# Attention and a maxout feed-forward on one core: the order in which the weights are prepared, and the engine that scales p in the first two batches

## The chip, the cores and the metric

The kernel runs on one core of one Trainium2 chip. The metric is the device time of one execution in microseconds (us); lower is better. The time before is the median of three runs, 803.49 us (803.19 to 803.58).

## The reference

Eight batches of eight-head attention over 576 positions, with a window of 128 keys and a linear bias by distance, and then a feed-forward layer on all 4608 tokens, whose hidden value is the largest of three products. Cut to what matters:

```python
scores = scale * np.matmul(q, k.transpose(0, 1, 3, 2))         # q, k, v: (8, 8, 576, 64)
bias = slopes[:, None, None] * (-np.abs(rel).astype(np.float32))[None, :, :]
scores = np.where((rel >= 0) & (rel < 128), scores + bias[None], -1000000000.0)
attn = np.exp(scores - np.max(scores, axis=-1, keepdims=True))
attn = attn / (np.sum(attn, axis=-1, keepdims=True) + 1e-09)
x = np.matmul(attn, v) -> (4608, 512)
h = np.maximum(np.maximum(x @ w1, x @ w2), x @ w3)              # w1, w2, w3: (512, 768)
return h @ w_out                                                # w_out: (768, 512)
```

## The kernel before

**Attention.** The work is cut into tasks (a batch and a pair of heads, `t` = 0 to 31, four to a batch) and steps (128 queries of a task, `s` = 0 to 159, five to a task, the fifth with 64 queries). For a pair of steps `products` (L314) makes the scores on the tensor engine (PE). For each step `score` masks them on the vector engine (DVE, L329 or L332), adds the bias and finds the row minimum of the negated scores (DVE, L344), and takes exp on the scalar engine (ACT, L348), which leaves p and its row sums. `sums_of` turns the sums into reciprocals on DVE (L357, L360), into the tile `st`. `normalise` multiplies p by them: before the change on ACT, one instruction for each head of a step (L367). `turn` transposes p on PE (L376), copies it out of PSUM on ACT (L380, L386, L389), and GpSimd (POOL) cuts the two triangles out of it (L390, L394). `mix` multiplies with v on PE (L416), and after a task's last step ACT copies the result into `xk` (L425).

**Feed-forward.** It runs one batch behind attention. Batch 0 is multiplied plainly, in 88 units (`plain_unit`, L585): 8 for each of 12 groups of weights. Groups 0 to 8 are the thirds of w1, w2, w3 for one part p of the hidden rows; groups 9 to 11 are w_out. Its operand `xs` is cut from `xk` (ACT L442, DVE L443) when all of batch 0's attention is done. The outputs of groups 0 to 8 are merged by `put`: the first third of a part is copied by ACT (L546), the others are max-ed by DVE (L544). Batches 1 to 7 run a scheme with seven products in place of eight (`unit`, L623); it needs sums and differences of the weights, which `add` and `add_part` make on DVE (L195, L153) from a copy of the weights in device memory, `w32`.

**Preparing the weights.** The weights come in as 64-bit values. The generator `preparing` walks over the groups in the order of the table `A_ORDER`, four steps to a group: two of `convert` (ACT L138 and L142, DVE L139, L143 and L148 for each, and a store to `w32`, L149), and two of `part` (a high and a low half by ACT L152 and DVE L153; into the ring `wt` for groups 0 to 8, which the plain units read, and into the constant tiles `ow` for groups 9 to 11). The ring has room for three groups, so the parts of groups 3 to 8 wait until the plain units have used up the group that stands three before. After that come 36 steps of `add` and `add_part` in the order of `B_ORDER`. `weights(n, upto)` takes n steps, and more if fewer than `upto` are done. It is called once at each attention step by the loop at L691 and L692 (s = 1 to 25), and by the units: one step at every second plain unit, and as many as the unit's own group needs (L569).

**What sets the order.** All calls are put into one list of events with a time in steps (L641 to L692) and emitted in that order; the framework's scheduler then moves instructions within each engine, until the `fix` event in batch 2 holds PE's to the written order. Each engine works through its own instructions in order. SP issues the loads and stores.

Of the kernel before, what the change touches and what calls it, by code (L numbers as in the profile page):

```python
# [13 lines left out]
ALU = mybir.AluOpType  # L14
# [15 lines left out]
def attention_maxout_kernel(  # L30
# [11 lines left out]
    nc = tc.nc  # L42
    P = 128
    B, NP, _, _, S = qk.shape
# [41 lines left out]
        out=prev, in_=prev, pattern=[[1, P]], compare_op=ALU.is_gt, fill=0.0,  # L86
# [42 lines left out]
    def fetch(g):  # L129
        for j in range(2):  # L130
            raws[g, j] = hs_p.tile([P, 2 * DM], I32, name="hs2", bufs=4)
            nc.sync.dma_start(raws[g, j], w_all[g, j].bitcast(I32))
# [82 lines left out]

        return (n - RING, 6 if a else 3) in used

    A_ORDER = [0, 1, 2, 9, 10, 11, 3, 4, 5, 6, 7, 8]
    B_ORDER = [0, 1, 2, 9, 10, 11, 3, 4, 5, 6, 7, 8]

    def preparing():
        fetch(A_ORDER[0])
        fetch(A_ORDER[1])
        for n, g in enumerate(A_ORDER):
            for j in range(2):
                convert(g, j)
                yield
            while 3 <= g < 9 and (g - 3, "plain") not in used:
                yield True
            for c in range(2):  # L230
                part(g, c)
                yield
            if n + 2 < NG:
                fetch(A_ORDER[n + 2])
        for g in B_ORDER:
            while g < 2 and (8, "plain") not in used:
                yield True
            while 2 <= g < 9 and not ahead(9 + g, 1):
                yield True
            while g >= 9 and (10, "plain") not in used:  # L240
                yield True
            add(g)
            yield
            for a in range(2):
                add_part(g, a)
                yield
# [5 lines left out]
    def weights(n=0, upto=0):  # L252

        nonlocal prepared
        while n > 0 or prepared < upto:
            stuck = next(steps_of_weights, True)
            if stuck:
                assert prepared >= upto or prepared == STEPS, (prepared, upto)
                return
            prepared += 1  # L260
            n -= 1
# [100 lines left out]
    def normalise(t, i):  # L362
        n = rows[i]
        st, two = stats[t, i // 2]
        for a, p in enumerate(two):
            for j in range(2):
                nc.scalar.activation(p[:n, j], p[:n, j], AF.Copy, scale=st[:n, 2, a, j:j + 1])  # L367

# [192 lines left out]
    def plain_unit(v):  # L561
# [6 lines left out]
        i, j = ij = ((0, 0), (0, 1), (1, 0), (1, 1))[o]  # L568
        weights(r % 2, 4 * (A_ORDER.index(g) + 1) if g < 9 else 48)  # L569
        if g < 9:  # L570
# [70 lines left out]
    def at(when, what, *args):  # L641
        events.append((when, len(events), what, args))
# [3 lines left out]
    for t, (b, hp) in enumerate(tasks):  # L646
        for i in range(NB):
            s = t * NB + i + shift[b]
            if i == LOAD_I and t + 2 < len(tasks):
                at(s - 0.4, load, t + 2)  # L650
            if i == NB - 1 and t + 1 < len(tasks):
                at(s - 0.4, load_v, t + 1)
            if i == 0 and 0 < t < NP:
                at(s - 1, slopes, t)
            c = s - (t * NB + i) % 2

            if s == c:
                at(c + 0.002, products, t * NB + i)
                at(c + LAG_T + 0.003, turn, t * NB + i)
            at(s + 0.04, score, t, i)  # L660
            if i % 2 or i + 1 == NB:
                at(s + 0.9, sums_of, t, i)
                at(s + 1.3, normalise, t, i)
            e = t * NB + next(min(e + 1, NB - 1) for e in GROUPS if e >= i)
            at(e - e % 2 + shift[b] + LAG_X + 0.001, mix, t, i)
# [23 lines left out]
    for u in range(77 * B, 77 * B + 3):  # L689
        at(when, unit, u)  # L690
    for s in range(1, n_steps + LAG_X):  # L691
        at(s + 0.2, weights, 1)  # L692

    def fix():
        nonlocal fixed
# [48 lines left out]
```

## Time and profile before

| | before |
|---|---|
| median of three runs | 803.49 us |
| profiled execution, its own time | 799.82 us |
| its span, from first to last instruction | 797.7 us |
| PE busy | 759.2 us (95%) |
| weight loads of PE busy | 674.2 us (85%) |
| DVE busy | 559.9 us (70%) |
| ACT busy | 531.3 us (67%) |
| POOL busy | 166.8 us (21%) |

The profile shows one execution; its rows name the line of the kernel, the engine, the operation, the tile written and read, and the shapes. Busy time counts the time in which at least one instruction of the engine runs; two neighbours overlap a little, so busy time and count give the duration of one instruction, and the distance from start to start gives what one costs an engine that is never idle. An engine's wait is put down to what released it last. In the strip of 40 slices a digit is a tenth of 20 us. Line numbers are those of the kernel before; below the changed lines those of the kernel after are 5 to 6 higher.

### The profile page before, as it was taken

The page shows a single profiled execution, that of the slowest core. Times are in us where ns is not written, and L with a number is a line of the kernel's source. Part 1 is how long each engine was busy: PE and PEld are TensorE (multiplying, and loading weights), DVE is VectorE, ACT ScalarE, POOL GpSimd, SP SyncE. Part 2 cuts the span into 40 slices and gives each one's busy share as a digit, 9 for nine tenths or more (in the row PEclk, how much of TensorE's full clock was granted, in tenths as well). Part 3 has the DMA queues.
Part 4 walks back from the last instruction along what each step waited for, and adds up shares of the span by engine and source line. Part 5 has one row for each costly group of instructions (what it writes and reads, how often), then busy time and mean ns, then how long its engine had stood idle before and what let it go on. Part 6 is the DMA issues. An engine that isn't in the chain of part 4 may idle for free.

```text
span 797.7 us, 18112 instructions
## 1 busy us (share of the span) xinstructions
PE 759.2 (95%) x6344; PEld 674.2 (85%) x6344; DVE 559.9 (70%) x1897; ACT 531.3 (67%) x1736; POOL 166.8 (21%) x374
## 2 busy tenths in 40 slices
PE   4776998999999999999999999999999999999987
PEld 2434987998888998899989999898988999899987
DVE  5677888488999757793777747793777747673662
ACT  6888888568878656775667657676667667552332
POOL 1221111111214122221223122221222122201100
PEclk7756999999999999999999999999999999999999
DMA  8775785387899459864887459864788458755951
GB/s 282 266 243 171 228 302 208 115 297 231 318 329 314 166 196 320 286 215 138 285 295 252 162 187 323 282 234 136 277 285 257 160 195 288 245 198 195 301 181 60
DMA packets 53771, 187.96 MB, mean 236 GB/s; under 512 B 5936, under 2 KB 14896, under 8 KB 46768
## 3 DMA queue, kind: packets, MB, share of 16 engines
q0 software_dynamic: 15552, 99.10, 37.6%
q1 hardware_dynamic: 37984, 87.64, 32.0%
q8 instruction: 50, 0.82, 0.4%
q14 instruction: 41, 0.34, 0.1%
q10 hardware_dynamic: 144, 0.07, 0.0%
HBM read 154.53 MB, written 32.24 MB: 234 GB/s over the span
## 4 chain that ended last, share of the span: by engine, by line
PE 65%; DVE 12%; issue 9%; ACT 6%; DMA 4%; POOL 2%; SPq 0%; POOLq 0%; ACTq 0%; DVEq 0%
PE ps_m L623 44%; PE ps_x L416 6%; PE ps_m L585 6%; PE ps_s L314 5%; PE pt L376 4%; DMA wt<-keep 2%; ACT p L348 2%; DVE hs L443 2%; DVE xs L443 2%; DMA hs<-in_w_all 1%; DVE t L549 1%; DVE s L344 1%; DVE ps_s L332 1%; DVE hq L550 1%; ACT xs L442 1%
## 5 line engine op out<-in xcount | busy, mean ns | idle before, releaser
L623 PE MATMUL ps_m<-xs,wt 128*128 128x288 f32 x2646 | 370.4, 297 | 4.1 <-DMA wt<-keep 1.7
L623 PEld LDWEIGHTS ps_m<-xs,wt 128*128 128x128 f32 x2646 | 355.4, 188 | 7.9 <-DVE t L549 3.8
L390 POOL TENSOR_SCALAR_AFFINE_SELECT pp<-pr 128x256 f32<-128x256 f32 (+1 forms) x128 | 54.7, 428 | 401.9 <-ACT pr L389 220.2
L348 ACT ACTIVATE p<-s,st 128x128 f32<-128x128 f32 (+1 forms) x320 | 127.0, 399 | 16.0 <-DVE st L344 14.6
L632 ACT COPY t<-ps_m 128x288 f32<-128x288 f32 x231 | 89.7, 394 | 71.2 <-PE ps_m L623 70.8
L623 PE MATMUL ps_m<-hs,ow 128*128 128x288 f32 x882 | 124.0, 297 | 1.6 <-DVE hs L443 0.8
L367 ACT ACTIVATE p<-p,st 128x128 f32<-128x128 f32 (+1 forms) x320 | 110.5, 396 | 19.4 <-DVE st L360 19.4
L623 PEld LDWEIGHTS ps_m<-hs,ow 128*128 128x128 f32 x882 | 118.7, 188 | 3.1 <-ACT t L632 1.2
L270 POOL DMA_DIRECT2D wt<-keep x108 | 58.3, 539 | 194.3 <-PE ps_m L623 187.7
L344 DVE CUSTOM_DVE_ANT_0 s<-ps_s,bias 128x128 f32<-128x128 f32 (+1 forms) x300 | 76.7, 281 | 17.4 <-PE ps_s L314 13.6
L416 PE MATMUL ps_x<-pp,v 128*64 128x256 f32 (+3 forms) x768 | 81.3, 339 | 3.7 <-POOL pp L390 3.6
L332 DVE COPY_PREDICATED ps_s<-prev,ps_s 128x256 f32<-128x256 uint8 x120 | 50.8, 423 | 46.2 <-PE ps_s L314 44.7
L549 DVE TENSOR_TENSOR t<-ps_m,t 128x288 f32<-128x288 f32 x126 | 56.5, 452 | 36.3 <-PE ps_m L623 24.2
L314 PE MATMUL ps_s<-qk 64*64 64x192 f32 (+1 forms) x1080 | 70.2, 336 | 9.2 <-DVE st L344 5.0
L416 PEld LDWEIGHTS ps_x<-pp,v 128*64 128x64 f32 (+1 forms) x768 | 46.1, 142 | 29.9 <-issue 10.6
L442 ACT CAST hs<-hq 128x288 fp32r<-128x288 f32 x117 | 49.0, 430 | 31.9 <-DVE hq L550 16.5
L376 PE MATMUL pt<-ident,p 128*128 128x128 f32 (+1 forms) x320 | 59.2, 296 | 11.2 <-ACT p L367 7.1
L376 PEld LDWEIGHTS pt<-ident,p 128*128 128x128 f32 (+1 forms) x320 | 34.8, 146 | 40.3 <-issue 18.9
L585 PE MATMUL ps_m<-xs,wt 128*128 128x288 f32 x432 | 63.3, 306 | 3.3 <-DVE xs L443 2.6
L585 PEld LDWEIGHTS ps_m<-xs,wt 128*128 128x128 f32 x432 | 60.6, 196 | 4.2 <-DVE xs L443 3.0
L314 PEld LDWEIGHTS ps_s<-qk 64*64 64x64 f32 x1080 | 41.1, 138 | 26.7 <-issue 10.5
L389 ACT COPY pr<-pt 128x256 f32<-128x256 f32 x64 | 18.9, 321 | 66.5 <-PE pt L376 66.5
(58 smaller groups left out, 849.4 us busy)
## 6 DMA issues: line engine op xcount, KB each, us to landing
wt<-keep POOLq DMA_DIRECT2D x54, 1024.0 KB, 7.3
wt<-keep POOLq DMA_DIRECT2D x54, 768.0 KB, 5.5
qk<-in_qk SPq DMA_DIRECT2D x31, 576.0 KB, 5.8
hs<-in_w_all SPq DMA_DIRECT2D x24, 512.0 KB, 5.0
v<-in_v SPq DMA_DIRECT2D x32, 320.0 KB, 4.6
keep<-wt SPq DMA_DIRECT2D x36, 256.0 KB, 3.8
outT<-t SPq DMA_DIRECT2D x64, 144.0 KB, 1.8
wt<-keep SPq DMA_DIRECT2D x27, 256.0 KB, 4.2
```

The lines of the kernel that those rows point to most:

```text
L270: nc.gpsimd.dma_start(wts[n, a], keep[n % 9][a])
L314: pe(nc.tensor.matmul(ps[j][d:d + D, o:o + k1 - k0], lhsT=qkt[t][j * D:(j + 1) * D, 0, q0:q0 + D], rhs=qkt[t][j * D:(j + 1) * D, 1, k0:k1] ...
L332: nc.vector.copy_predicated(both[:, :, P:], mask.unsqueeze(1).broadcast_to([n, 2, P]), both[:, :, :P],)
L344: nc.vector.tensor_tensor_reduce(out=s[:n], in0=ps[j][:n, P:2 * P], in1=(bias if i else bias0)[:n, 2 * hp + j, :], scale=-0.125, scalar=3. ...
L348: nc.scalar.activation(p[:n, j], s[:n], AF.Exp, bias=st[:n, 0, a, j:j + 1], scale=-1.0, accum_out=st[:n, 1, a, j:j + 1])
L367: nc.scalar.activation(p[:n, j], p[:n, j], AF.Copy, scale=st[:n, 2, a, j:j + 1])
L376: pe(nc.tensor.transpose(out=pt[:, a, j, :n], in_=p[:n, j], identity=ident[:n, :n]))
L416: pe(nc.tensor.matmul(x[j * D:(j + 1) * D, c:c + e - a], lhsT=vv[:n, i, j * D:(j + 1) * D], rhs=w[:n, j].rearrange("p a b -> p (a b)")[:, ...
L549: nc.vector.tensor_tensor(out=s, in0=ps, in1=e, op=ALU.add)
L585: pe(nc.tensor.matmul(ps, lhsT=lt, rhs=rt, start=m == 0 and c == 0, stop=m == len(pairs) - 1, skip_group_check=True,))
L623: pe(nc.tensor.matmul(ps, lhsT=lt, rhs=rt, start=i == 0 and k in (0, 1, 4), stop=i == len(pairs) - 1, skip_group_check=True,))
L632: nc.scalar.copy(out=e, in_=ps)
```

## The change

Three edits. (1) `A_ORDER`, the order in which the groups of weights are prepared, becomes 0 to 11; before, groups 9 to 11 stood between 2 and 3. (2) The preparing step at each attention step stops after s = 11; before, it went on to s = 25, so that 25 steps (groups 0, 1, 2, 9, 10, 11 and one step of group 3) were asked for in the first 25 attention steps, and now 11 are (groups 0 and 1 and three of the four steps of group 2). The rest is asked for by the plain units. (3) For the tasks of the first two batches (`t < 2 * NP`) p is scaled on DVE, by one multiplication for both heads of a step, with the reciprocals of `st` broadcast along the row; the other batches keep the two ACT instructions.

```diff
-    A_ORDER = [0, 1, 2, 9, 10, 11, 3, 4, 5, 6, 7, 8]
+    A_ORDER = [0, 1, 2, 3, 4, 5, 6, 7, 8, 9, 10, 11]
...
         for a, p in enumerate(two):
+            if t < 2 * NP:
+                nc.vector.tensor_tensor(
+                    out=p[:n], in0=p[:n], in1=st[:n, 2, a].unsqueeze(2).broadcast_to([n, 2, P]), op=ALU.mult
+                )
+                continue
             for j in range(2):
                 nc.scalar.activation(p[:n, j], p[:n, j], AF.Copy, scale=st[:n, 2, a, j:j + 1])
...
     for s in range(1, n_steps + LAG_X):
-        at(s + 0.2, weights, 1)
+        if s < 12:
+            at(s + 0.2, weights, 1)
```

The order of the instructions changes on every engine but POOL in the part of the program up to the end of batch 0's plain units. On PE the rows differ only within the attention of batch 0 and the first plain units; from there on the two kernels give PE the same instructions in the same order.

First ACT, in the later half of batch 0's attention. `p` is exp's output and its scaling, `pt` the transposed p, `ow` the prepared weights of groups 9 to 11, and `hs` the raw weights: hs_434 belongs to group 9 and hs_567 to group 10 in the kernel before, hs_425 to group 3 and hs_845 to group 4 in the kernel after. Before:

```order
L152 CAST ow_122<-hs_434 128x256
L152 CAST ow_124<-hs_434 128x256
L348 ACTIVATE p,st<-s,st 128x128 x2
L138 ACTIVATE hs_567<-hs_567 128x512
L367 ACTIVATE p<-p,st 128x128 x4
L142 ACTIVATE hs_567<-hs_567 128x512
L389 COPY pr<-pt 128x2x64
L348 ACTIVATE p,st<-s,st 128x128
L386 COPY pp<-pt 128x2x128
```

After:

```order
L142 ACTIVATE hs_425<-hs_425 128x512
L348 ACTIVATE p,st<-s,st 128x128 x2
L138 ACTIVATE hs_845<-hs_845 128x512
L385 COPY pr<-pt 128x512
L348 ACTIVATE p,st<-s,st 128x128 x5
L394 COPY pr<-pt 128x2x64
L348 ACTIVATE p,st<-s,st 128x128
L391 COPY pp<-pt 128x2x128
L348 ACTIVATE p,st<-s,st 64x128 x2
L430 COPY xk_715<-ps_x 128x576
```

The scaling of p (L367) and the parts of groups 9 to 11 (L152 into `ow`) are gone from this place; conversions of groups 3 and 4 stand there in their stead, fewer of them.

Second DVE, in the plain units of groups 7 and 8. The rows that write `hq` (L544 before, L549 after) take the maximum with a unit's product; hs_1740 and hs_1742 are the raw weights of group 10, hs_1863 those of group 11. Before:

```order
L544 TENSOR_TENSOR hq<-ps_m_1881,hq 128x288
L544 TENSOR_TENSOR hq<-ps_m_1899,hq 128x288
L544 TENSOR_TENSOR hq<-ps_m_1940,hq 128x288
L544 TENSOR_TENSOR hq<-ps_m_1954,hq 128x288
L544 TENSOR_TENSOR hq<-ps_m_1968,hq 128x288
L443 TENSOR_TENSOR hs_2024<-hq,hs_2024 128x288
L344 ISA s,st<-ps_s,bias_115 128x128
```

After:

```order
L148 TENSOR_TENSOR hs_1740<-hs_1740 128x512
L549 TENSOR_TENSOR hq<-ps_m_1812,hq 128x288
L148 TENSOR_TENSOR hs_1742<-hs_1742 128x512
L153 TENSOR_TENSOR ow_118<-hs_1740,ow_118 128x256
L549 TENSOR_TENSOR hq<-ps_m_1856,hq 128x288
L153 TENSOR_TENSOR ow_119<-hs_1740,ow_119 128x256
L153 TENSOR_TENSOR ow_122<-hs_1742,ow_122 128x256
L153 TENSOR_TENSOR ow_124<-hs_1742,ow_124 128x256
L549 TENSOR_TENSOR hq<-ps_m_1880,hq 128x288
L139 SCALAR_TENSOR_TENSOR hs_1863<-hs_1863 128x512
L448 TENSOR_TENSOR xs<-xt,xs 128x576
L549 TENSOR_TENSOR hq<-ps_m_1900,hq 128x288
```

Where five maxima followed each other, the preparation of groups 10 and 11 now stands between them.

## The prediction

> **What bounds the kernel now.** I read the strip of 40 slices first, to find the stages that are not alike.
>
> ```profile
> ACT  6888888568878656775667657676667667552332
> PEclk7756999999999999999999999999999999999999
> ```
>
> A digit is 20 us. The first four slices differ from all others: PE's granted clock is 0.5 to 0.7, and ACT is at its highest. From slice 5 on PE has its full clock. So I cut the span at the places that matter and asked for the windows: start and end, length, then the busy time of PE, PEld, DVE, ACT and POOL, PE's clock, DMA share, GB/s.
>
> ```profile
> 8.00:75.00 67.00, 45.73 (x281) 22.82 (x281) 48.78 (x193) 58.11 (x195) 12.81 (x32) 0.64 0.74 249
> 75.00:133.00 58.00, 54.93 (x460) 49.56 (x461) 48.32 (x152) 50.27 (x150) 8.26 (x18) 0.94 0.74 252
> 133.00:161.00 28.00, 28.00 (x244) 24.90 (x246) 15.09 (x56) 16.12 (x56) 5.45 (x14) 0.99 0.36 117
> 161.00:185.00 24.00, 24.00 (x211) 22.90 (x202) 19.49 (x64) 17.25 (x55) 3.60 (x6) 1.00 0.84 273
> 185.00:260.00 75.00, 73.90 (x654) 65.68 (x653) 71.07 (x247) 61.25 (x203) 16.97 (x32) 1.00 0.90 310
> ```
>
> The first row is the head: attention of batch 0 alone, until the first plain unit. The next three are batch 0's plain units (groups 0 to 5, 6 to 8, 9 to 11), the last the sums of weights during batch 1. PE is full from 133 us on and nearly full before; only in the head is it idle for long. What it waits for there, in all, how often and longest, from the waits of PE, and the row in the timeline that ends the head:
>
> ```profile
> PE pt L376 <- ACT p L367: 7.1, 2, 4.6
> PE pt L376 <- ACT pr L380: 4.1, 3, 1.6
> PE ps_x L416 <- POOL pp L390: 3.6, 4, 1.0
> PE ps_m L585 <- DVE xs L443: 2.6, 1, 2.6
> 74.89 7.36 PE L585 MATMUL ps_m<-xs,wt 128*128 128x288 f32 x42 [2.59 <-DVE xs L443]
> ```
>
> The two largest are behind ACT's queue, and ACT is busy for 58.1 of 67 us (87%). The head is ACT's. Everything after it is PE's, in an order that the change leaves alone from the first plain units on, so an earlier end of the head moves the end of the kernel, unless a later stage gives it back.
>
> **The head, priced.** The groups that the change touches there, busy and mean ns of one, ACT first, then DVE; the third row is the scaling of p alone, by windows.
>
> ```profile
> L138 ACT ACTIVATE hs<-hs 128x512 int32<-128x512 uint32 x12 | 7.9, 658 | 1.7 <-DMA hs<-in_w_all 1.7
> L152 ACT CAST ow<-hs 128x256 fp32r<-128x256 f32 x10 | 3.7, 393 | 0.0
> 8.00:75.00 67.00, 13.07 (x40) 0.64 0.74 249
> L148 DVE TENSOR_TENSOR hs<-hs 128x512 f32<-128x512 f32 x12 | 8.5, 705 | 0.8 <-ACT hs L142 0.7
> L153 DVE TENSOR_TENSOR ow<-hs,ow 128x256 fp32r<-128x256 f32 x10 | 4.4, 460 | 1.2 <-ACT ow L152 1.2
> ```
>
> Neighbours overlap, so I price by the distance from start to start, from the timeline:
>
> ```profile
> 11.70 0.65 ACT L138 ACTIVATE hs<-hs 128x512 int32<-128x512 uint32 x1
> 12.25 0.67 ACT L142 ACTIVATE hs<-hs 128x512 int32<-128x512 f32 x1
> 56.87 1.26 ACT L367 ACTIVATE p<-p,st 128x128 f32<-128x128 f32 x4
> 80.23 0.69 DVE L139 SCALAR_TENSOR_TENSOR hs<-hs 128x512 int32<-128x512 int32 x1 [0.56 <-ACT hs L138]
> 80.84 0.68 DVE L148 TENSOR_TENSOR hs<-hs 128x512 f32<-128x512 f32 x1
> 81.44 0.42 DVE L143 TENSOR_SCALAR hs<-hs 128x512 int32<-128x512 int32 x1
> 53.72 0.75 DVE L153 TENSOR_TENSOR ow<-hs,ow 128x256 fp32r<-128x256 f32 x2
> ```
>
> ACT: 0.55 for a conversion; (1.26 - 0.39)/3 = 0.29 for a scaling, and as much for a cast into ow. DVE: 0.61, 0.60 and 0.34 (0.42 less the same overlap) for L139, L148 and L143; 0.34 for an L153 of 256 columns.
>
> ACT loses all 40 scalings, 40 x 0.29 = 11.6 us. Of the 24 conversions ahead of the last xs cut 17 are left in the new order (groups 9 to 11 out, group 3 and one instruction of group 4 in): 7 x 0.55 = 3.9. The ten casts into ow go: 10 x 0.29 = 2.9. Sum 18.4, so 58.1 becomes 39.7.
>
> DVE gains 21 multiplications. No row shows one; the nearest is L153, with two fp32 inputs in SBUF and 256 columns, 0.34; as ends I keep half of L143's 0.34, 0.17, and L139's 0.61 (either moves the sum by less than 6 us, inside the bounds below). I take L153's 0.34, the row of the same size and kind: 7.1 us. It loses 3 x 0.61 + 4 x 0.34 + 5 x 0.60 = 6.2 of conversions and 10 x 0.34 = 3.4 of ow. Net -2.5: 48.8 becomes 46.3.
>
> So DVE becomes the fullest engine of the head, with PE at 45.7 close behind. If DVE were used as well as ACT was (87%), the head would last 46.3/0.87 = 53.2 us, 13.8 less. If it stayed at its present share (48.8/67 = 73%), 63.6, 3.4 less. Three engines of nearly equal load hinder each other more than one full one, but the wait for ACT between the reciprocal and the transpose goes, since both are now on DVE. I take 10 us, nearer to the upper end, with 3.4 to 13.8 for the range.
>
> One row speaks against the multiplications. POOL's cuts of p take 0.41 us, but 0.86 where DVE runs an operation with two SBUF inputs, which is itself drawn out from 0.69 to 0.90:
>
> ```profile
> 39.42 0.90 DVE L148 TENSOR_TENSOR hs<-hs 128x512 f32<-128x512 f32 x1
> 39.73 0.86 POOL L394 TENSOR_SCALAR_AFFINE_SELECT pp<-pr 128x256 f32<-128x256 f32 x1
> ```
>
> A meeting costs 0.45 us on POOL. Such conversions leave the head (3 L139, 5 L148, 10 L153) as 21 multiplications come, so the number of meetings hardly rises, and I add nothing. The Trainium skill, SBUF — State Buffer, section "Who interferes with whom", says that a DVE instruction with two SBUF inputs and a GpSimd instruction that reads SBUF shut each other out; this row agrees, and if each of the 21 met a cut the head would lose another 9 us.
>
> **The plain units.** PE's waits from 75 to 185 us, and the scalings there:
>
> ```profile
> PE ps_s L314 <- DVE st L344: 2.4, 1, 2.4
> PE ps_m L585 <- ACT hq L546: 0.7, 1, 0.7
> 75.00:133.00 58.00, 10.07 (x30) 0.94 0.74 252
> 133.00:161.00 28.00, 4.63 (x14) 0.99 0.36 117
> ```
>
> Both waits end chains through ACT, at 50.3 of 58 us. It loses 30 x 0.29 = 8.7 there, and DVE gains 15 x 0.34 = 5.1 and loses the rest of groups 11 and 3 that it still had. Of 3.1 us I take back 2 (0 to 3.1).
>
> From 133 to 161 DVE gets groups 9 to 11: six conversions of 1.55 us and twelve parts of 0.34, 13.4 us, and 7 multiplications, 2.4. 15.1 + 15.8 = 30.9 us in 28, if nothing overlaps; its 56 instructions stand alone now and would each give up some 0.08 in a dense queue, which leaves 26.4. That is 94 to 110% of the window: a loss of 0 to 2.9 us on PE, through the maxima (L544) that free its PSUM. I take 0.5. That DVE can be that full at little cost is shown by the last window: 71.1 of 75 us, and PE waited for DVE and ACT for
>
> ```profile
> PE ps_m L623 <- ACT t L632: 0.6, 1, 0.6
> PE ps_m L623 <- DVE wt L153: 0.4, 1, 0.4
> ```
>
> In that same window lies the risk: what DVE brings along from 161 us, and the first load from w32, which SP now issues behind the stores of group 11, meets a DVE with 4.5 us to spare up to 185 and 3.9 after it. 0 to 3.9; I take 1. Everything later is as before.
>
> **Sum.** 10 + 2 - 0.5 - 1 = 10.5 us. The profiled execution took 799.82 us (span 797.7, 2.1 around it): 789.3. The median is 3.7 above that execution, so I forecast 793.0.
>
> **Rivals.** *PE's clock sets the head.* PE was busy for 45.7 us at a clock of 0.64; of its waits above none but the first (4.6) was longer than 2.6. If the clock falls to 0.5, the same work takes 45.73 x 0.64/0.5 = 58.5 us, and with the 6.2 us of waits for POOL and xs the head lasts 64.7: 2.3 gained, some 2 with the later terms, and 801.5. For it: the low clock has been there in all four slices. Against: PE now waits less, and the clock was 0.94 and more as soon as it was dense.
>
> *The head runs freely.* A denser PE gets the full clock, its work falls to 29.3 us, DVE is used at 87%: 13.8 + 3.1 = 16.9 with nothing given back, 786.6. The Trainium skill, TensorE: Matmul & The Clock Gate, Part 1, has the clock full after a busy window of some 3.4 us and halved only after an idle one as long; by that rule one wait of 4.6 us and the rest of 2.6 or less would have cost the head its clock once, early, and this case would be the likely one. The trace's 0.64 speaks against the rule, so I give it little.
>
> *DVE bounds what follows, and the kernel gets slower.* From 75 to 260 us DVE was busy for 154.0 of 185. The change adds 22 multiplications (7.5) and the 13.4 us of groups 9 to 11, less 3.8 that lay behind 75 us before (group 3's two conversions, 1.55 each, and the last two parts into ow): 17. If DVE's 31 us of idleness are waits that stay, every one of these lengthens the stretch: 17 - 11 = 6 us slower (the head's 10 and 1 of the plain units gained), 809.5. It decides once that idleness takes up less than 6 of the 17. For it: from 185 on DVE is at 95%. Against: in 133 to 161, where most of it lands, DVE is idle for 12.9 us, and there PE was not late once.
>
> **How the numbers follow.** Forecast 0.68; the clock 0.14; the free head 0.10; DVE the bound 0.08. A measurement can tell about 0.2%, 1.6 us, from no change. Faster: the forecast, the free head and over half of the clock's case, 0.86; same: the rest of it, 0.06; slower 0.08. The range, 786 to 801, takes in the forecast's own bounds (gains of 3 to 17) and most of the free head and the clock's case; it leaves out the slower rival and the tails, some 0.17.
>
> **What would show it.** The first long row of plain products near 65 us instead of 74.9; ACT near 40 us busy in the head and DVE near 46; L367 on DVE at 0.34 us from start to start; no PE wait for ACT's p; DVE above 90% in the window of groups 6 to 8 with PE waits under 3 us; and behind the sums of weights the same trace, earlier by the gain. I am wrong if PE's first plain unit comes after 71 us, or if PE's waits between it and the end of batch 1's sums grow by more than 5 us.

## The result, and the profile after

| | before | after |
|---|---|---|
| median | 802.59 us (9 runs, 797.96 to 803.58) | 796.32 us (9 runs, 791.66 to 798.58) |
| profiled execution, span | 799.82, 797.7 us | 798.58, 796.9 us |
| a second profiled execution, span | | 792.84, 791.1 us |

The ratio is 0.994, 95% interval 0.9912 to 0.9967: between 2.6 and 7.1 us faster (0.0033 and 0.0088 of 802.59). The forecast was 793.0, a gain of 10.5. The second profiled execution comes from an experiment below; without it the first would have misled.

The strip of 40 slices of the kernel after:

```profile
ACT  5664768678888656775677656775666656642332
PEclk9766999999999999999999999999999999999999
```

ACT's first four digits fell from 6, 8, 8, 8 to 5, 6, 6, 4; PE's clock in the third and fourth is still 0.6. The windows of before, now after the change (same columns):

```profile
8.00:75.00 67.00, 49.53 (x308) 27.65 (x309) 46.08 (x197) 42.00 (x141) 15.46 (x32) 0.74 0.59 200
75.00:133.00 58.00, 55.30 (x481) 49.51 (x484) 50.24 (x171) 41.36 (x121) 11.82 (x22) 0.98 0.76 253
133.00:161.00 28.00, 26.78 (x237) 23.64 (x230) 25.30 (x75) 20.24 (x61) 5.21 (x10) 1.00 0.72 242
161.00:185.00 24.00, 22.71 (x187) 21.42 (x187) 19.44 (x67) 19.32 (x62) 2.55 (x6) 1.00 0.87 290
185.00:260.00 75.00, 74.06 (x657) 66.23 (x657) 72.36 (x252) 61.50 (x204) 17.70 (x32) 1.00 0.91 314
```

The loads of the head came out as worked: ACT 42.0 (39.7 forecast), DVE 46.1 (46.3). In groups 6 to 8 DVE is at 25.3 of 28 us. PE's waits in the head:

```profile
PE ps_x L421 <- POOL pp L395: 5.9, 7, 1.7
PE pt L381 <- ACT hs L142: 4.8, 1, 4.8
PE ps_s L314 <- DVE st L344: 4.6, 3, 2.1
PE pt L381 <- ACT pr L385: 1.3, 2, 0.7
```

Of the 7.1 us for ACT's scaling the 4.6 of the first transposes stayed: it is 4.8 now and put down to a conversion. The waits for `pr` fell from 4.1 to 1.3, those for POOL's cuts rose from 3.6 to 5.9. The timeline has the multiplication's price and the start of the steady plain products:

```profile
33.22 0.74 DVE L367 TENSOR_TENSOR p<-p,st 128x256 f32<-128x256 f32 x2
33.89 0.15 DVE L357 TENSOR_SCALAR st<-st 64x2 f32<-64x2 f32 x1
...
73.09 1.33 PE L590 MATMUL ps_m<-xs,wt 128*128 128x288 f32 x4 [0.25 <-DVE xs L448]
```

(33.89 - 33.22)/2 = 0.335 us for one, as priced. The steady products start at 73.09, not near 65; in the second execution they do so at 69.91:

```profile
69.91 2.26 PE L590 MATMUL ps_m<-xs,wt 128*128 128x288 f32 x15 [0.66 <-DVE xs L448]
```

A few plain products run earlier now, between the attention's, so the start of the first is no mark. I take the start of the product that comes behind the first n feed-forward products on PE (all L585 and L623 products counted, L590 and L628 after), and call it the n-th: the 48th ends the head (group 0's eight units of six products), the 288th group 5, the 432nd group 8, the 650th lies in the sums of weights. (Of the 88 plain units 72 belong to groups 0 to 8 and 16 to w_out; it is not eight for each of twelve groups.)

| gain in us | forecast | first execution | second |
|---|---|---|---|
| head (to the 48th: 84.16 before, 80.17 and 75.06 after) | 10 | 4.0 | 9.1 |
| to the 288th (49.62; 47.51, 47.37) | 2 | 2.1 | 2.2 |
| to the 432nd (27.88; 29.61, 29.21) | -0.5 | -1.7 | -1.3 |
| to the 650th (36.89; 38.14, 37.93) | -1 | -1.3 | -1.0 |
| sum | 10.5 | 3.1 | 9.0 |

From the 650th product to the 3700th the gain stays within 0.3 us. At the end of batch 7 both executions give back 2 us more. PE's waits from 725 us on add up to 3.4 us before and to 5.1 and 5.5 after; of these, 1.7, 2.5 and 3.0 are waits for streamed weights, and the rest are waits for DVE. The row of the first execution:

```profile
L628 PE MATMUL ps_m<-xs,wt 128*128 128x288 f32 x2646 | 370.8, 297 | 5.9 <-DMA wt<-keep 2.5 <-ACT t L637 1.0 <-DVE t L554 1.0
```

In seven of the eleven edited kernels below the gain at the last product was within 0.2 us of that at the 3700th; in the other four (scaling alone, weights behind, scaling 20 to 33, unread multiplication) 1.0 to 3.3 us were given back. No kernel was seen both ways, so it is not shown whether this goes with the execution or with the edit.

### The profile page after: what moved, and what is told of

Its sections match the earlier page's. It is cut to its first block, busy times and chain, and to the rows that moved or that the text cites. A ratio compares the mean times of both kernels' runs of the same rounds, so it can differ in the third digit from the quotient of the medians.

```text
span 796.9 us, 18059 instructions
## 1 busy us (share of the span) xinstructions
PE 758.3 (95%) x6344; PEld 673.7 (85%) x6344; DVE 567.7 (71%) x1937; ACT 509.5 (64%) x1656; POOL 171.9 (22%) x374
## 4 chain that ended last, share of the span: by engine, by line
PE 56%; DVE 14%; issue 13%; DMA 8%; ACT 6%; POOL 2%; SPq 1%; POOLq 0%; ACTq 0%; DVEq 0%
PE ps_m L628 40%; PE ps_x L421 6%; PE ps_s L314 5%; DMA hs<-in_w_all 4%; PE pt L381 4%; DVE xs L448 2%; DVE hs L448 2%; ACT p L348 2%; DMA wt<-keep 1%; DMA w<-hs 1%; PE ps_m L590 1%; DVE t L554 1%; DVE ps_s L332 1%; DVE s L344 1%; DVE hq L555 1%
## 5 line engine op out<-in xcount | busy, mean ns | idle before, releaser
L628 PE MATMUL ps_m<-xs,wt 128*128 128x288 f32 x2646 | 370.8, 297 | 5.9 <-DMA wt<-keep 2.5
L628 PEld LDWEIGHTS ps_m<-xs,wt 128*128 128x128 f32 x2646 | 355.4, 188 | 10.1 <-DVE hq L555 2.7
L395 POOL TENSOR_SCALAR_AFFINE_SELECT pp<-pr 128x256 f32<-128x256 f32 (+1 forms) x128 | 56.3, 440 | 393.5 <-ACT pr L394 225.0
L628 PE MATMUL ps_m<-hs,ow 128*128 128x288 f32 x882 | 124.1, 297 | 2.0 <-DVE hs L448 1.2
L628 PEld LDWEIGHTS ps_m<-hs,ow 128*128 128x128 f32 x882 | 118.7, 188 | 3.5 <-DVE hs L448 1.4
L372 ACT ACTIVATE p<-p,st 128x128 f32<-128x128 f32 (+1 forms) x240 | 84.1, 397 | 18.3 <-DVE st L360 18.2
L590 PE MATMUL ps_m<-xs,wt 128*128 128x288 f32 x432 | 66.3, 309 | 3.0 <-DVE hq L549 2.7
L590 PEld LDWEIGHTS ps_m<-xs,wt 128*128 128x128 f32 x432 | 61.2, 197 | 6.1 <-DVE hq L549 3.2
L399 POOL TENSOR_SCALAR_AFFINE_SELECT pp<-pr 128x256 f32<-128x256 f32 (+1 forms) x128 | 64.0, 500 | 0.0
```

The lines of the kernel that those rows point to most:

```text
L399: nc.gpsimd.affine_select(out=w[:n, :, 0, :n], in_=r[:n, a, :, :n], pattern=[[0, 2], [1, n]], compare_op=ALU.is_ge, fill=0.0, base=0, chan ...
L590: pe(nc.tensor.matmul(ps, lhsT=lt, rhs=rt, start=m == 0 and c == 0, stop=m == len(pairs) - 1, skip_group_check=True,))
L628: pe(nc.tensor.matmul(ps, lhsT=lt, rhs=rt, start=i == 0 and k in (0, 1, 4), stop=i == len(pairs) - 1, skip_group_check=True,))
```

## The experiments

The traces after the change raised the question where 6 of the head's 10 us went. **Theory 1**: the multiplications make DVE's queue, with the conversions in it, the bound of the head's first half. **Theory 2**: PE at half clock bounds its second half. **Rivals**: meetings of DVE and POOL, PE's clock throughout, ACT's load. The expectations were written with the start of step 12 (its first exp on ACT) as the mark between the halves.

To read the head in the end I cut it where the instructions mean the same in every kernel: at the copy of the second task's result into `xk` (end of the second task's attention) and at that of the fourth (end of batch 0's attention). The first part starts at 8 us. One profiled execution of each; the ratio is against the kernel before, from all runs.

| kernel | first part | second part | 48th product at | median, ratio (95%) |
|---|---|---|---|---|
| before | 36.25 | 28.17 | 84.16 | |
| after | 34.53 | 28.12 | 80.17 | 796.32, 0.994 (0.9912 to 0.9967) |
| after, again | 33.05 | 26.41 | 75.06 | 792.84 (one run) |
| weights alone | 35.51 | 25.04 | 76.52 | 794.28, 0.991 (0.9877 to 0.9942) |
| scaling alone | 32.36 | 30.85 | 80.45 | 797.13, 0.9951 (0.9929 to 0.9973) |
| scaling from step 12 | 35.27 | 24.98 | 77.27 | 791.84, 0.9875 (0.9841 to 0.9908) |
| one SBUF input | 34.66 | 26.55 | 80.58 | 798.2, 0.9949 (0.9919 to 0.9978) |
| weights late | 26.59 | 26.36 | 70.55 | 788.45, 0.9838 (0.9797 to 0.9879) |
| weights behind | 35.25 | 25.84 | 77.62 | 794.64, 0.9938 (0.9906 to 0.997) |
| scaling 20 to 33 | 34.27 | 21.91 | 73.42 | 793.92, 0.9915 (0.9884 to 0.9946) |
| extra products | 35.63 | 25.63 | 78.49 | 795.09, 0.9933 (0.9901 to 0.9966) |
| weights late, ACT | 26.69 | 23.61 | 71.12 | 791.76, 0.9888 (0.9855 to 0.9922) |
| unread multiplication | 36.58 | 20.68 | 74.28 | 790.95, 0.9873 (0.9829 to 0.9916) |
| late, from step 12 | 27.29 | 22.65 | 68.32 | 793.03, 0.9886 (0.9847 to 0.9925) |

**Weights alone**: the kernel after without the branch for `t < 2 * NP` in `normalise`.

> The new order and the shorter preparation, with p of all batches scaled by ACT as before. Theory 1 (DVE's queue: in the kernel after, the multiplications stand behind the conversions in DVE's in-order queue, so the first 12 steps of the head came 4 us later and only the last 12 gained 8): ACT loses 6.8 us of conversions and casts here and nothing is put on DVE, which loses 9.6 us; the 48th feed-forward product comes about as early as in the kernel after or earlier (4 to 8 us ahead of before), the first transposes as in before. Rival (PE's clock of 0.64 holds the head, whatever ACT and DVE do): the 48th product within 2 us of before. Rival (meetings of the multiplications with POOL's cuts ate the gain): the head gains the whole 6.8/0.87 = 8 us. All three expect the groups 6 to 8 to give back about 1.7 us, as in the kernel after, and the total 1 to 6 us under before.

**Scaling alone**: the kernel before with that branch.

> The old order of the weights, and p of the first two batches scaled by DVE. Theory 1 (DVE's queue): DVE gets 7.1 us on top of its 48.8 in the head and becomes its fullest engine (55.9 of 67 us); the multiplications wait behind the conversions of all of the head, so it gains at most 1 us and may lose 4 (the 48th product 1 earlier to 4 later). Rival (ACT was the head's bound, and 11.6 us less of it pay wherever they are): the 48th product 5 us or more earlier. Rival (PE's clock): within 2 us, with the same clock of 0.6. In the stretch from the first plain unit to the end of group 5, 2 us gained as in the kernel after, in all theories.

With the scaling alone the 48th product came 3.7 us earlier, between the two forecasts (at most 1 by theory 1, 5 or more by the rival on ACT). Alone, the order brought 7.2 us (0.009 of 801.99) and the scaling 3.9; together they brought 4.8 (0.006 of 802.59). They don't add up.

**Scaling from step 12**

```diff
-            if t < 2 * NP:
+            if 12 <= t * NB + i < 2 * NP * NB:
```

> The kernel after, but DVE scales p only from step 12 on; steps 0 to 11, beside which the weights are prepared, are scaled by ACT as before. Theory 1 (DVE's queue): the 4 us that the first 12 steps lost come back, the 48th product is 6 to 8 us ahead of before (in the kernel after 4.0), and step 12 starts at 40 us or earlier (44.2 in the kernel after, 39.4 before). Rival (PE's clock): the 48th product as in the kernel after, within 1 us. Rival (meetings with POOL's cuts): about half of the multiplications are gone, so half of what was missing (6 us) comes back, evenly over the head and not in its first half alone.

Step 12 started at 39.26 as theory 1 expected, the 48th product came 6.9 us ahead of before, and the ratio lies under that of the kernel after. I took theory 1 as shown here, which was too early. The mark was at fault. ACT in the kernel after, and then with the weights alone, around step 12's first exp:

```profile
43.58 0.67 ACT L447 CAST xs<-xk 128x576 fp32r<-128x576 f32 x1
44.16 0.40 ACT L348 ACTIVATE p<-s,st 128x128 f32<-128x128 f32 x1
```

```profile
38.69 0.54 ACT L389 COPY pr<-pt 128x256 f32<-128x256 f32 x2 [0.89 <-PE pt L376]
39.12 0.41 ACT L348 ACTIVATE p<-s,st 128x128 f32<-128x128 f32 x1
```

After the change the scheduler has put the second copy into `xk` (42.53 us) and the first cut of `xs` ahead of that exp; with the weights alone that copy comes at 43.51, behind it. By the copy, work of one meaning, the kernel after is 1 to 2.5 us ahead at this point, not 5 behind.

**One SBUF input**

```diff
-                nc.vector.tensor_tensor(
-                    out=p[:n], in0=p[:n], in1=st[:n, 2, a].unsqueeze(2).broadcast_to([n, 2, P]), op=ALU.mult
-                )
+                for j in range(2):
+                    nc.vector.tensor_scalar(
+                        out=p[:n, j], in0=p[:n, j], scalar1=st[:n, 2, a, j:j + 1], scalar2=None, op0=ALU.mult
+                    )
```

> The kernel after, with each multiplication of DVE (two heads, two SBUF inputs, 256 columns) replaced by two of one head (one SBUF input and a scalar for each row, 128 columns). Rival (meetings of DVE's two-input instructions with POOL's cuts ate the head's gain): the cuts in the head take about 0.41 us each instead of 0.44 to 0.50, and the 48th product comes 2 us or more earlier than in the kernel after. Theory 1 (DVE's queue): two instructions of 0.17 to 0.25 us cost what one of 0.34 cost, and the 48th product stays within 1 us of the kernel after (4.0 us ahead of before). PE's clock: no change.

POOL's cuts did not get shorter (the two of a step took 565 and 482 ns on average in the head, 504 and 527 in the kernel after) and the head stayed as it was (the 48th product at 80.58 and 80.17). So this does not clear the meetings. In the kernel after the longest cuts of the head lie beside a run of DVE's preparing steps, not beside the multiplication:

```profile
61.25 1.26 POOL L395 TENSOR_SCALAR_AFFINE_SELECT pp<-pr 128x256 f32<-128x256 f32 x1 [2.93 <-ACT pr L385]
62.47 2.01 POOL L399 TENSOR_SCALAR_AFFINE_SELECT pp<-pr 128x256 f32<-128x256 f32 x1
...
61.56 0.68 DVE L153 TENSOR_TENSOR wt<-hs,wt 128x512 fp32r<-128x512 f32 x1
...
62.58 0.41 DVE L143 TENSOR_SCALAR hs<-hs 128x512 int32<-128x512 int32 x1
62.92 0.68 DVE L139 SCALAR_TENSOR_TENSOR hs<-hs 128x512 int32<-128x512 int32 x1
63.52 0.68 DVE L148 TENSOR_TENSOR hs<-hs 128x512 f32<-128x512 f32 x1
```

Two cuts of 0.41 took 1.26 and 2.01: 2.5 us, about what PE's wait for POOL grew by (2.3). In the second execution the same two took 1.24 and 2.00.

**Weights late**

```diff
-        if s < 12:
+        if s >= 12:
```

> The kernel after, with the preparation at the attention steps moved from s = 1 to 11 to s = 12 to 25: the first half of the head has the multiplications on DVE and no conversions, the second half has both. Theory 1 (the multiplications lose the first half because they stand in DVE's queue beside conversions): without them the loss is gone, step 12 starts at 38 us or earlier (39.1 to 39.4 in the kernels that scale by ACT there, 44.2 in the kernel after), and the second half becomes longer by 3 us or more than the 26.5 of the kernel after. Rival (the loss is the multiplication itself: DVE has to wait for exp, multiply, and only then goes on to the next scores, whatever else stands in its queue): step 12 starts at 42 us or later. Rival 2 (the second half is PE's at half clock): the second half takes 26 to 30 us all the same, and the 48th product comes 5 us or more earlier than in the kernel after.

Step 12 started at 32.60 and the 48th product at 70.55. By the marks that hold:

```profile
8.00:34.59 26.59, 22.50 (x153) 10.71 (x153) 19.35 (x104) 17.65 (x69) 7.03 (x16) 0.87 0.46 164
34.59:60.95 26.36, 17.37 (x113) 8.57 (x112) 19.29 (x77) 18.30 (x57) 10.94 (x16) 0.61 0.79 261
```

The first part is 8 us shorter than after the change (6.5 than in its second execution). The scheduler has moved some of the preparation forward again: of the 43 preparing instructions that ACT and DVE run in the first part of the kernel after, 13 are still there. The second part, which now holds 30 instead of 10, is no longer than after the change; but it has lost something too, as the section on the prediction shows. This kernel has the lowest median: 13 us under before, and its interval lies apart from that of the kernel after.

**Weights behind**

```diff
-            at(s + 0.2, weights, 1)
+            at(s + 0.35, weights, 1)
```

> The kernel after, with the preparing steps of the head emitted just behind the multiplications instead of just ahead of them (s + 0.35 in place of s + 0.2), so that on DVE most of them stand ahead of the conversions of their step. Same instructions. Theory 1 in its narrow form (a multiplication waits behind the conversions of its own step): 3 us or more of the 4 lost in the first half come back, step 12 starts at 41 us or earlier (44.2 in the kernel after), the 48th product about 7 us ahead of before instead of 4.0. Theory 1 in its wide form (DVE's load of conversions and multiplications together, in whatever order): step 12 starts at 42 to 45 us, the 48th product within 1.5 us of the kernel after.

Step 12 at 44.92, the first part 35.25 (34.53 and 33.05 in the kernel after): the other order on DVE brought nothing back.

**Scaling 20 to 33**

```diff
-            if t < 2 * NP:
+            if 20 <= t * NB + i < 34:
```

> The kernel after, but DVE scales p only for steps 20 to 33, which lie in the plain units of groups 0 to 5; the head and the units of groups 6 to 11 scale on ACT as before. If the sum by stages that the runs show so far adds up: the head as with the weights alone (48th product 7.6 us ahead of before), 3 more by the end of group 5 (10 ahead), and only 0.2 given back in groups 6 to 8 where the kernel after gives back 1.7: 9 to 10.5 us ahead of before at the 600th product, a time of 790 to 792. Rival (what the multiplications gain in groups 0 to 5 is given back in any case, since PE only runs ahead to the next wait for weights): 7 us ahead at the 600th product, as with the weights alone, 794.

10.7 us ahead at the 48th product, 13.9 at the 288th, 9.0 at the 600th: what groups 0 to 5 gained was given back although ACT scaled again, the rival's case. That the 9.0 lies in the first forecast too is luck: the head was 3.1 us further ahead than with the weights alone.

**Extra products** on top of the weights alone:

```diff
+    idle = ps_m.tile([P, 512], F32, name="ps_m2")
...
+            nc.tensor.matmul(
+                idle[:, :256], lhsT=bias[:, 0], rhs=bias[:, :2].rearrange("p h c -> p (h c)"),
+                start=True, stop=True, skip_group_check=True,
+            )
...
+                if t < NP:
+                    at(c + 0.0025, busy, 4)
+                    at(c + LAG_T + 0.0035, busy, 4)
```

> The weights alone (p scaled by ACT), with 8 further matrix products for each pair of attention steps of batch 0 (bf16, 128 x 128 by 256 columns, into a PSUM bank that nothing reads in the head): 80 in all, extra work whose result is not used. With the weights alone PE was busy for 26.2 of the 29.4 us from step 12 to the end of batch 0's attention, at a granted clock of 0.54, and the chain of waits there is mostly PE. Theory 2 (the second half of the head is PE's, at half clock): if the extra products lift the clock to 0.8 or more, PE's own work falls to some 18 us there and the 48th product comes 3 us or more earlier than with the weights alone (76.5 us), in spite of some 4 us of extra products. If the clock stays at 0.5, the extra products (some 0.2 us each, 16 us in all) make the head longer by 5 us or more: the half is then PE's too, and only the clock can't be lifted so. Rival (PE's clock is of no account): the head stays within 2 us of the weights alone in either case.

All 80 ran before 28 us, 76 of them in the first part, so only that part was tried. The extra products first, then the weights alone:

```profile
8.00:43.63 35.63, 30.35 (x239) 17.79 (x231) 26.48 (x115) 30.65 (x107) 7.40 (x16) 0.87 0.82 282
```

```profile
8.00:43.51 35.51, 25.12 (x156) 12.51 (x157) 25.78 (x110) 30.33 (x106) 6.60 (x16) 0.68 0.81 281
```

PE was busy for 5 us more at a clock of 0.87 instead of 0.68, and the part stayed as it was: more load and a higher clock together did not move it. The two executions of the kernel after say the same of the clock alone: 34.53 us at 0.81 and 33.05 at 0.64. The 48th product came 2 us later than with the weights alone, at a second part of 25.63 (25.04).

**Weights late, ACT**: the weights alone with `s >= 12`; and **after, again**, unchanged.

> The preparation of weights at s = 12 to 25 and p of all batches scaled by ACT: with the kernel that scales by ACT and prepares at s = 1 to 11 (step 12 starts at 39.1 us), the kernel after (both in the first half, 44.2) and the one that prepares late and scales by DVE (32.6) this completes a table of two by two. Theory 1 in its wide form (DVE's load of conversions and multiplications together): with the conversions gone DVE has room, so who scales matters little: step 12 starts at 31.6 to 33.6 us, and the multiplication's 5 us are lost only where conversions stand beside it. Rival (ACT's load sets the first half): 12 steps of scaling put 24 x 0.29 = 7 us on an ACT that is busy for 16.8 of 24.6 us there, and step 12 starts at 34.5 us or later. Rival (the multiplication is dear in itself): step 12 starts at 30 us or earlier. For the time: 787 to 790 by theory 1, 790 to 793 by the rival on ACT.

> The kernel after once more, for the spread of its own trace. If the reading by stages holds, step 12 starts at 43 to 45 us again and the 48th feed-forward product comes at 76 to 81 us (80.2 in the first trace); PE's granted clock in the second half of the head may be anything from 0.5 to 1 in a stretch of 4 us, since the kernels with the same work there showed 0.54 and 0.77, and the 48th product should be the later the lower it is. If step 12 moved by more than 2 us between two runs of one kernel, the differences of 4 us on which theory 1 rests would be of no use.

The first two windows of the kernel with late weights and ACT:

```profile
8.00:34.69 26.69, 21.92 (x172) 10.64 (x172) 16.39 (x98) 23.17 (x93) 5.53 (x16) 0.94 0.50 177
34.69:58.30 23.61, 15.72 (x104) 8.37 (x108) 18.24 (x65) 22.60 (x74) 6.70 (x16) 0.67 0.74 252
```

Step 12 started at 30.24, between theory 1 (31.6 or later) and the multiplication as dear in itself (30 or earlier); the time, 791.76, is the one that the rival on ACT named, whose step 12 (34.5 or later) did not come.

So the two by two of the first part is 35.5 and 34.5 or 33.1 with the weights early (ACT scales, DVE scales), 26.7 and 26.6 with the weights late. Preparing early costs 6.5 to 9 us there; who scales makes 0 to 2.5. The other kernels of the table fit in: with the weights early 34.3 to 36.6 where ACT scales the first part and 32.4 to 35.3 where DVE does, with the weights late 26.6 to 27.3.

Not all of this reaches the 48th product. The rest of the head, with ACT scaling, in the kernel with late weights and in the one with early weights:

```profile
58.30:71.12 12.82, 11.04 (x75) 10.06 (x67) 10.36 (x30) 11.18 (x32) 0.00 (x0) 0.68 0.73 236
```

```profile
68.55:76.52 7.97, 7.97 (x71) 7.41 (x65) 6.48 (x19) 7.97 (x24) 0.00 (x0) 1.00 0.43 127
```

Late weights give back 4.9 us here, and the 48th product comes 5.4 us earlier, not 9. Where DVE scales it comes 9.6 or 4.5 us earlier, depending on the execution of the kernel after.

The kernel after came 5.1 us earlier at the 48th product in its second trace than in its first: 1.5 in the first part, 1.7 in the second, 1.9 behind it. The last stretch of the head, from the fourth copy into `xk` to the 48th product, in the first and then in the second:

```profile
70.65:80.17 9.52, 9.27 (x62) 7.97 (x54) 6.06 (x21) 7.01 (x19) 0.00 (x0) 0.65 0.23 69
```

```profile
67.46:75.06 7.60, 6.94 (x61) 5.80 (x54) 6.06 (x21) 7.00 (x19) 0.00 (x0) 0.93 0.30 85
```

This is the same work, with PE at 0.65 and at 0.93; the second part ran at 0.68 and at 0.69.

**Unread multiplication** (the weights alone; for steps 0 to 11 DVE multiplies `dist` by the reciprocals into a tile that nothing reads yet, and ACT scales):

```diff
+            if t * NB + i < 12:
+                nc.vector.tensor_tensor(
+                    out=ow[0][:n, 0, 0].rearrange("p (j c) -> p j c", j=2), in0=dist[:n].unsqueeze(1).broadcast_to([n, 2, P]),
+                    in1=st[:n, 2, a].unsqueeze(2).broadcast_to([n, 2, P]), op=ALU.mult
+                )
```

> The weights alone (p scaled by ACT, preparation at s = 1 to 11), with one more DVE multiplication for each of steps 0 to 11, of the size and kind of the scaling and reading the same reciprocals, into a tile that nothing reads yet: extra work that nobody waits for. Theory 1 as the runs so far leave it (the first half goes by DVE's load: in ten kernels DVE was busy for 71 to 81% of it whatever ACT had, so that a microsecond more on DVE makes it about a microsecond longer): 12 x 0.34 = 4.1 us more, step 12 starts at 42 to 45 us as in the kernel after (44.2 and 42.7), against 39.1 with the weights alone. Rival (it is the chain: in the kernel after PE's transposes wait for the multiplication, which waits for exp; work that nobody waits for costs little): step 12 starts at 41 us or earlier.

Step 12 started at 40.62 and the first part grew by 1.1 us, for 3.8 more of DVE (29.5 against 25.8). With this base a microsecond more on DVE is not a microsecond more of the first part. But ACT scales here and is busy for 30.7 of 36.6 us (84%), and in the kernel after for 23.4 of 34.5 (68%) with DVE the fuller; so for the kernel after theory 1 in its last form was not tried.

This run, the weights alone, the extra products and the scaling of 20 to 33 have all but the same instructions in the second part. Their rows, in the order extra products, weights alone, scaling 20 to 33, unread multiplication:

```profile
43.63:69.26 25.63, 23.78 (x126) 11.27 (x125) 8.98 (x51) 16.06 (x62) 5.54 (x16) 0.50 0.20 68
```

```profile
43.51:68.55 25.04, 23.19 (x125) 10.96 (x124) 9.00 (x51) 16.02 (x63) 5.52 (x16) 0.50 0.21 69
```

```profile
42.27:64.18 21.91, 19.02 (x126) 9.46 (x125) 8.69 (x51) 16.07 (x62) 5.53 (x16) 0.73 0.23 79
```

```profile
44.58:65.26 20.68, 17.80 (x127) 9.55 (x128) 8.51 (x46) 16.05 (x61) 5.54 (x16) 0.75 0.27 88
```

DVE, ACT and POOL have the same work to 0.5 us, and the stretch takes 25 us at a clock of 0.50 and 21 to 22 at 0.73 to 0.75. PE's busy time makes the difference (23 to 24 us against 18 to 19); its idle time is 2 to 3 us in all four. So with preparation and scaling off DVE, PE and its clock set the second part. No run set the clock there: this rests on four traces that differ in it by themselves.

**Late, from step 12**: weights late, with `if 12 <= t * NB + i < 2 * NP * NB`.

> Preparation at s = 12 to 25, and DVE scales p for steps 12 to 39: in the first half neither conversions nor multiplications are on DVE, in the second half ACT, which was busy for 32.1 of 34 us with late preparation and scaling by ACT, is relieved of the scalings. If each half goes by its fullest engine: step 12 starts at 30 to 31 us (30.2 with late preparation and scaling by ACT), the 48th product comes 13 to 16 us ahead of before, and the time is 785 to 788 us, ratio 0.980 to 0.984. Rival (the second half is PE's at half clock and POOL's cuts: it takes 28 us whatever ACT has): the 48th product 12 to 13.5 us ahead of before, the time as with late preparation and scaling by DVE, 788.5.

In its trace the head is the shortest of all, 15.8 us ahead at the 48th product, and its profiled execution took 786.15 us; but the other five took 791.8 to 796.4, and the median is no better than that of late weights with ACT. The late kernels' medians lie 788 to 793 with intervals that overlap; where the other executions lose what the profiled one gained, no trace shows.

## Why the prediction came out as it did

The direction was right, and 796.32 lies inside the stated 786 to 801; the gain is 6.3 us by the medians (4.8 by the ratio) where 10.5 was forecast. Two terms were mis-sized. One is "Everything later is as before": both executions gave back 2 us at the end of batch 7. The other is the head, in "I take 10 us, nearer to the upper end": it brought 4.0 us in one execution and 9.1 in the other, both inside the stated 3.4 to 13.8, and which of them stands for the median no trace shows. That step applied one share of use, ACT's 87%, to a DVE that takes ACT's place, and to the whole head at once. The runs showed parts that are limited differently.

The terms between the head and the 650th product came out in size: 2 us were gained in groups 0 to 5 (2.1 and 2.2) and some given back behind them (3.0 and 2.4, forecast 1.5). That does not show their reasons, and the agreement may be luck. In groups 0 to 5 three kernels in which ACT scales throughout gained 1.6 to 2.6 us as well (extra products, weights late with ACT, unread multiplication), and the weights alone lost 0.4.

**The first part kept what holds it up.** Of 36.25 us it lost 1.7 and 3.2, though ACT lost 8 us of work there:

```profile
8.00:44.25 36.25, 25.70 (x164) 12.77 (x164) 26.50 (x111) 31.50 (x109) 6.62 (x16) 0.68 0.80 276
44.25:72.42 28.17, 19.92 (x118) 9.94 (x116) 19.70 (x74) 24.03 (x80) 6.19 (x16) 0.57 0.64 209
```

```profile
8.00:42.53 34.53, 23.38 (x145) 11.93 (x149) 26.55 (x111) 23.39 (x77) 7.32 (x16) 0.81 0.75 262
42.53:70.65 28.12, 22.05 (x149) 12.57 (x147) 16.48 (x79) 15.22 (x57) 8.13 (x16) 0.68 0.43 141
```

(before, then after). The change leaves the preparation of groups 0 to 2 there, and DVE is as busy as before. Taking most of it out is worth 6.5 to 9 us there whoever scales. That is shown; why it costs so much is not. The order on DVE (weights behind) and PE's clock (extra products, and the two executions of the kernel after) are ruled out. Two things on record point further. PE's first transposes waited 4.6 us in one piece before, 4.8 and 5.1 after and 4.3 with the weights alone, and with the weights late no wait of PE in the first part is longer than 2.1. And ACT, which works in order, stood still until the first conversion's weights had come, 1.7 us before and 3.1 after, with the next exp behind it though DVE had its minimum ready at 9.1 us:

```profile
11.69 0.65 ACT L138 ACTIVATE hs<-hs 128x512 int32<-128x512 uint32 x1 [3.05 <-DMA hs<-in_w_all]
12.24 0.39 ACT L348 ACTIVATE p<-s,st 128x128 f32<-128x128 f32 x1
```

One reading of all first parts stays untested: the fullest engine sets each. Where ACT scales, ACT is busy for 84 to 89% of the part, in eight kernels; where DVE scales, DVE is busy for 73 to 81%, in six executions. By it the prediction's method was sound for this part and its 87% too high for DVE: DVE's 26.5 us at 87% would be 30.5 us, and 34.5 and 33.1 were measured.

**The second part lost its ACT work and went hardly faster.** ACT fell from 24.0 to 15.2 us and the part from 28.2 to 28.1, or 26.4. In part this is because of where the marks lie. After the change 17 of the head's 48 plain products run in this part (L590 alone), and before none did:

```profile
42.53:70.65 28.12, 5.05 (x17) 3.45 (x17) 0.68 0.43 141
```

They are missing from the rest of the head, which took 11.7 us before and 9.5 and 7.6 after. The second part and this rest together took 39.9 us before and 37.6 and 34.0 after, 33.0 with the weights alone, and 36.0 and 36.4 with the weights late (DVE scales, ACT scales). What is late next in the second part is POOL's cuts, by PE's waits, and, as I read the four rows above, PE at a low clock; but the two executions of the kernel after differ by 1.7 us here at the same clock, so for this kernel the clock's share is argued, not shown.

```profile
PE ps_x L421 <- POOL pp L395: 4.4, 4, 1.7
```

(PE's waits in the second part, kernel after; 1.8 before, 3.7 in the second execution.) I had set those meetings at nothing because their number would hardly rise; it was the length of two that rose.

So the rival in which PE's clock sets the head, given 0.14, has the right mechanism for the second part where ACT scales, if not its time: its 0.5 was seen there. (Its gain of 2.3 us and the forecast's own later terms add up to 2.8, which gives 800.7 and not 801.5.) By the Trainium skill, TensorE: Matmul & The Clock Gate, Part 1, the clock is full after some 3.4 us of sustained work and halved only after an idle window as long. With the weights alone PE was recorded busy for 23.2 of 25.0 us at 0.50, without a break from 43.51 to 50.00, so the measurement decides here against taking recorded busy time for that work. The free head did not come: PE's waits for POOL grew and the clock was 0.74. Nor did the slower rival: from 75 to 260 us DVE's work grew from 154.0 to 167.3 us, and the stretch from the 288th to the 650th product by 3.0 and 2.4. With the weights alone DVE's work there was 167.2 us, and that stretch grew by 0.4 only; with the scaling of 20 to 33 it grew by 4.9. So DVE's load by itself is not what lengthens it, and what does stays open.

Of my own signs of being wrong, "PE's first plain unit after 71 us" came true in one execution of two (73.09, 69.91): one trace could not decide it. The two executions are 5.1 us apart at the 48th product, which is about the whole gain.

What stays open: why scaling only from step 12 gave a ratio under that of the kernel after (0.9875 and 0.994, intervals just apart), when the traces' heads, 77.3 against 80.2 and 75.1, do not separate them.

## What to carry to other kernels

Work moved out of a stage pays only where it was holding that stage up: split the stage where its load changes before applying a share of use, and ask of each part what is late next. Here the same preparing steps cost 6.5 to 9 us in the first part of the head; moved to the rest of it they cost 3.4 us where ACT scales (36.4 against 33.0) and between 2 us more and 2 less where DVE does (36.0 against 34.0 and 37.6). So the place of what stayed mattered as much as what left. Compare kernels at marks that a scheduler does not reorder, count what has crossed them, and take a second trace of the same kernel before reading differences of a few microseconds.

## What the runs showed of the hardware

The granted clock of one program differed between executions in the same stretch (0.65 and 0.93 above; 0.81 and 0.64 in the first part), and with the weights alone it stayed at 0.50 for 25 us with PE recorded busy for 93% of it. With 76 further bf16 products of 128 x 128 by 256 columns (mean 291 ns) it was 0.87 in the first part, without them 0.68; as one program alone shows 0.64 to 0.81 there, it is not shown that they lifted it. A POOL cut beside three DVE instructions in a row took 2.01 us instead of 0.41. With a one-input DVE multiplication the cuts were about as long (565 and 482 ns) as with a two-input one (504 and 527).
